# Re-ordered attention and maxout kernel: part of W loaded ahead of batch 1's x, single PSUM banks, padded x for every state read

## The chip, the cores and the metric

One core of one Trainium2 chip runs the program. The metric is device microseconds of one execution, as the median of several runs; less is better.

## The reference

Eight batches (B = 8) of attention between x and 32 state vectors per head, in both directions, and then a feed-forward layer whose hidden value is the largest of three products. H = 8 heads, S = 512 tokens, Ns = 32 states, D = 64.

```python
x:     (8, 8, 512, 64)      state: (8, 8, 32, 64)
a  = softmax(x @ state^T / 8, over the states);  xread = a  @ state     # 512 rows a batch
a2 = softmax(state @ x^T / 8, over the tokens);  sread = a2 @ x         # 32 rows a batch
y = concat([xread, sread], rows), heads side by side                    # (8*544, 512)
h = max(y @ w1, y @ w2, y @ w3)                                         # (8*544, 768)
out = h @ w_out                                                         # (8*544, 512), float32
```

## The kernel before

**What is computed where.** xread is never built. For a batch b the kernel multiplies each head's 32 states by the matching 64 rows of w1, w2, w3 ahead of time: G[b] holds state @ W for all heads, 128 rows (4 heads of 32 states) by 2 parities of heads by 3 matrices by 768 columns. Layer 1 is then aT @ G: for each of the six slices m of 128 hidden columns, `maxout` (L473) runs three PSUM banks (one for each matrix) of two 128x512 matmuls each. `max_first` (L489) copies the first bank to SBUF on ACT, `max_second` (L494) and `max_third` (L499) take the maximum with the second and the third bank on DVE, and the last writes ht. Layer 2 (L511) multiplies 128 tokens of ht by w_out in six 128x512 matmuls, `layer2_out` copies the bank to osb, and `store` sends osb to DRAM.

**The steps of a batch**, by the names that the plan uses: x is loaded with a cast to bf16 by POOL's DMA queue (`lx`; `lxg` loads the four even or odd heads only; `lxu` and `cxu` load uncast and cast on DVE, for batch 0's first half). x is turned to xT on TensorE (`xt`, with the copy `xtc`) for batches 0 and 1, and by a transposing DMA on SP's queue (`xtd`) for the rest. `sc` makes the scores (16 matmuls, or 8 for one parity), `ex` takes exp on ACT, `sum` adds over the states and inverts on DVE, `wt` multiplies (on POOL, 128x1024, or on DVE), giving a. a is turned by TensorE and a copy (`at`, `atc`) in batches 0 and 1, by DMA on SP's queue (`atd`) in the others. `sr` reads x by e for the 32 state rows (32 matmuls that use 32 columns of the array each), `srs` divides, `srt` turns the result by DMA on SP's queue, `ap` copies it to its place in atp, from which `l1s` makes the states' rows of layer 1 at the end. The states themselves are loaded in pairs of batches (`lst`), cast twice over (`stc`), turned (`stt` on TensorE) and copied into a block-diagonal tile bd (`stp`).

**G** is made by small matmuls on a quarter of the array, 64x32 (`g_mm`, L424): `g b m` makes slice m of all three matrices for batches 0 and 1, since W comes in slice by slice; `gr b c0 c1` makes 512 columns of the 2304 for the later batches, and `gq` 256. They are emptied by `gc`, `grc` and `gqc`.

**PSUM.** Four banks (tags b0 to b3) go to everything that takes one bank, in the order of the digits of BANKS. The other four are two pairs (w0, w1): `two_banks` gives a pair to `g`, to `gr` and to the scores of batches 2 to 7, and one instruction of 128x768 or 128x1024 empties the pair.

**sread's right side.** In batches 2 to 7 `pad` (L370) copies x on POOL into a tile xp with 65 columns a head, the 65th a one, so that one matmul of 65 columns gives the sum of e as well. In batches 0 and 1 the matmul takes 128 columns: 64 of x, and 64 ones that lie behind x in x_sb, by a hand-made address pattern (L389).

**What sets the order.** PLAN (L18) is a list of steps that one table of functions carries out; every engine does its own instructions in the order of that list, and waits only for its operands and for its buffer. BANKS, PAIRS and PLACES say which buffer each step takes. Each DMA stands in the queue of the engine that issues it (S is SP, P is POOL, A is ACT). `busy` is one matmul of zeros; these stand on TensorE ahead of the first use of W. At the end `look`, `flag` and `vl` test whether any sum left its range, in which case a second, safe program runs; `hold` is a matmul and a copy behind the last layer-2 copy.

In the plan the batches overlap: batch b's layer 1 stands with batch b-1's layer 2 and with batch b+1's G. The beginning is different: batches 0 and 1 are done together, slice by slice, as W lands.

Of the kernel before, what the change touches and what calls it, by code (L numbers as in the profile page):

```python
# [9 lines left out]
F32 = mybir.dt.float32  # L10
# [8 lines left out]
    lst 0 A; lxu 0 0 S; zero; clr 0; clr 1; clr 2; clr 3; warm; lxg 0 1; busy 1; xones 1; ident; busy 1;  # L19
    lxg 1 0; busy 1; busy 1; stc 0 D; busy 1; busy 1; busy 1; busy 1; busy 1; lxg 1 1; stt 0; busy 1; busy 1;  # L20
    cxu 0 0 D; xt 0 0; stp 0 A; busy 1; xt 0 1; lw 0 2 1; lw 0 1 0; xtc 0 0 D; sc 0 0; xones 0; lw 0 2 2;
    xtc 0 1 D; busy 1; busy 1; sc 0 1; xt 1 0; ex 0 0; ex 0 1; lw 1 3 0; sum 0 0; sum 0 1; xtc 1 0 A; busy 1;
    busy 1; xt 1 1; sc 1 0; xtc 1 1 D; ex 1 0; busy 1; busy 1; sc 1 1; lw 2 3 2; wt 0 1 D; lw 2 3 1; lw 3 4 0;
    wt 0 0 P; lw 3 6 2; at 0 0; sr 0; ex 1 1; sr 1; g 0 0; sum 1 0; wt 1 0 P; g 1 0; atc 0 0 A; at 0 1; at 1 0;
    gc 0 0 A; atc 0 1 A; g 1 1; sum 1 1; gc 1 0 D; atc 1 0 A; srs 0; srs 1; g 0 1; wt 1 1 P; at 1 1; gc 0 1 A;
    l1 0 0; atc 1 1 D; lst 1 A; m0 0 0; lst 3 A; gc 1 1 A; ma 0 0; lw 3 6 1; lw 4 6 0; lxg 2 1; lxg 2 0; l1 0 1;
    m0 0 1; lwo; mb 0 0; g 0 2; g 1 2; ma 0 1; l1 1 0; lst 2 A; gc 0 2 A; mb 0 1; m0 1 0; ma 1 0; l1 0 2;
    mb 1 0; gc 1 2 A; m0 0 2; ma 0 2; l1 1 1; m0 1 1; g 1 3; stc 1 P; mb 0 2; ma 1 1; g 0 3; mb 1 1; stt 1;
    gc 1 3 A; l1 1 2; gc 0 3 A; m0 1 2; stp 1 DA; ma 1 2; g 0 4; g 0 5; l1 0 3; gc 0 5 D; g 1 4; mb 1 2;
    gc 0 4 A; m0 0 3; gc 1 4 A; ma 0 3; gr 2 1792 2304; mb 0 3; l1 1 3; m0 1 3; grc 2 1792 2304 A; xtd 2;  # L30
    ma 1 3; l1 0 5; stc 2 P; g 1 5; gr 2 0 512; mb 1 3; m0 0 5; ma 0 5; l1 1 4; gc 1 5 A; gr 2 1280 1792;
    m0 1 4; grc 2 0 512 D; mb 0 5; gr 2 512 1024; ma 1 4; grc 2 1280 1792 AD; l1 0 4; m0 0 4; ma 0 4; stt 2;
    mb 0 4; sc 2 -; ex 2 -; grc 2 512 1024 D; stp 2 AD; stc 3 D; mb 1 4; l2 0 3; l2 0 0; l2c 0 3 A; l2c 0 0 A;
    sum 2 -; l2 0 1; ones; pad 2; lxg 3 0; lxg 3 1; wt 2 - P; stt 3; xtd 3; l2c 0 1 A; l1 1 5; pad 3;
    so 0 0 2 P; lx 4; m0 1 5; l2 0 2; ma 1 5; mb 1 5; stp 3 A; l2c 0 2 A; l2 1 0; gq 2 1024 1280; gr 3 0 512;
    gr 3 1792 2304; l2c 1 0 D; grc 3 1792 2304 D; gqc 2 1024 1280 A; grc 3 0 512 A; atd 2; sr 2; l2 1 1; srs 2;
    sc 3 -; l1 2 0; m0 2 0; ex 3 -; l2c 1 1 D; l2 1 3; ma 2 0; gq 3 1024 1280; so 0 2 4 P; gqc 3 1024 1280 A;
    l2c 1 3 A; gr 3 512 1024; gr 3 1280 1792; mb 2 0; sum 3 -; wt 3 - P; atd 3; xtd 4; srt 0; sr 3; srs 3;
    l1 2 1; m0 2 1; ma 2 1; l1 2 2; m0 2 2; mb 2 1; ma 2 2; l1 2 3; m0 2 3; mb 2 2; ma 2 3; l1 2 5; m0 2 5;
    mb 2 3; l2 1 2; grc 3 1280 1792 A; grc 3 512 1024 A; ma 2 5; mb 2 5; l2c 1 2 D; l1 2 4; so 1 2 4 P; m0 2 4;  # L40
    ma 2 4; lx 5; mb 2 4; so 1 0 2 P; pad 4; gr 4 1792 2304; gr 4 0 512; grc 4 1792 2304 AD; l2 2 0; l2 2 1;
    grc 4 0 512 D; l2c 2 0 A; l1 3 0; m0 3 0; sc 4 -; ex 4 -; xtd 5; l2c 2 1 D; l2 2 3; ma 3 0; gq 4 1024 1280;
    gr 4 1280 1792; gr 4 512 1024; mb 3 0; sr 4; gqc 4 1024 1280 A; sum 4 -; srs 4; l2c 2 3 A; l1 3 1; m0 3 1;
    ma 3 1; l1 3 2; m0 3 2; mb 3 1; ma 3 2; l1 3 3; m0 3 3; mb 3 2; ma 3 3; l1 3 5; wt 4 - P; m0 3 5; mb 3 3;
    l2 2 2; grc 4 1280 1792 A; grc 4 512 1024 A; ma 3 5; mb 3 5; l2c 2 2 D; l1 3 4; so 2 2 4 P; m0 3 4; ma 3 4;
    lx 6; mb 3 4; atd 4; srt 1; ap 0 A; so 2 0 2 P; pad 5; gr 5 1792 2304; gr 5 0 512; grc 5 1792 2304 AD;
    l2 3 0; l2 3 1; grc 5 0 512 D; l2c 3 0 A; l1 4 0; m0 4 0; sc 5 -; ex 5 -; xtd 6; l2c 3 1 D; l2 3 3; ma 4 0;
    gq 5 1024 1280; gr 5 1280 1792; gr 5 512 1024; mb 4 0; sr 5; gqc 5 1024 1280 A; sum 5 -; srs 5; l2c 3 3 A;
    l1 4 1; m0 4 1; ma 4 1; l1 4 2; m0 4 2; mb 4 1; ma 4 2; l1 4 3; m0 4 3; mb 4 2; ma 4 3; l1 4 5; wt 5 - P;
    m0 4 5; mb 4 3; l2 3 2; grc 5 1280 1792 A; grc 5 512 1024 A; ma 4 5; mb 4 5; l2c 3 2 D; l1 4 4; so 3 2 4 P;  # L50
    m0 4 4; ma 4 4; lx 7; mb 4 4; atd 5; srt 2; ap 1 A; so 3 0 2 P; pad 6; gr 6 1792 2304; gr 6 0 512;
# [20 lines left out]
    l2p 7 1 128 384; sop 7 2 0 128 A; l2p 7 0 256 384; l2pc s 0 0 256 A; l2pc 7 1 128 384 A; l2c s 1 D;  # L72
    l2p 7 1 384 512; l2p 7 0 128 256; sop 7 3 0 256 S; sop 7 2 128 384 P; l2pc 7 0 256 384 D; sop 7 1 128 384 A;
    l2pc 7 1 384 512 D; sop 7 1 384 512 A; l2pc 7 0 128 256 D; sop 7 0 128 256 A; sos 1 S; sop s 0 0 256 S;
    sop 7 0 256 384 S; hold; vl;
"""

BANKS = """
# [665 lines left out]
```

## Time and profile before

| | us |
|---|---|
| runs of the kernel (3): lowest, median, highest | 152.44, 152.61, 152.64 |
| span of the profiled execution | 150.5 |
| what lies around that span (median less span) | 2.1 |
| TensorE busy | 145.1 (96%) |
| VectorE (DVE) busy | 118.0 (78%) |
| ScalarE (ACT) busy | 83.2 (55%) |
| GpSimd (POOL) busy | 56.1 (37%) |

Times in the trace count from the start of the span. PE is TensorE's matmuls, PEld its weight loads. The granted TensorE clock was 1.000 over the span. A row of the chain of waits has a start, a length and what the time went to; a row of a timeline has a start, a length, the engine and the line, and in brackets how long that engine had been idle and what ended it. The length of a group of matmuls runs to the end of the last one, which overlaps with the next group; differences of starts don't have that overlap.

### The profile page before, as it was taken

The page shows a single profiled execution, that of the slowest core. Times are in us where ns is not written, and L with a number is a line of the kernel's source. Part 1 is how long each engine was busy: PE and PEld are TensorE (multiplying, and loading weights), DVE is VectorE, ACT ScalarE, POOL GpSimd, SP SyncE. Part 2 cuts the span into 40 slices and gives each one's busy share as a digit, 9 for nine tenths or more (in the row PEclk, how much of TensorE's full clock was granted, in tenths as well). Part 3 has the DMA queues.
Part 4 walks back from the last instruction along what each step waited for, and adds up shares of the span by engine and source line. Part 5 has one row for each costly group of instructions (what it writes and reads, how often), then busy time and mean ns, then how long its engine had stood idle before and what let it go on. Part 6 is the DMA issues. An engine that isn't in the chain of part 4 may idle for free.

```text
span 150.5 us, 3618 instructions
## 1 busy us (share of the span) xinstructions
PE 145.1 (96%) x1422; PEld 72.8 (48%) x1422; DVE 118.0 (78%) x202; ACT 83.2 (55%) x144; POOL 56.1 (37%) x78
## 2 busy tenths in 40 slices
PE   6998999999999999999999999999999999999991
PEld 2556443335444443444344434443444446689770
DVE  6488788999967899789978997899789888674443
ACT  3366888965654574457546764676466653332220
POOL 6996911090392507350735064506250200001500
PEclk9999999999999999999999999999999999999999
DMA  4999999949647996998399839983303340300555
GB/s 121 195 188 189 206 230 198 196 97 139 124 97 171 235 182 189 108 209 178 145 102 216 183 139 90 231 183 131 157 4 78 121 175 7 139 0 17 190 199 167
DMA packets 39108, 22.29 MB, mean 148 GB/s; under 512 B 23072, under 2 KB 36896, under 8 KB 39088
## 3 DMA queue, kind: packets, MB, share of 16 engines
q0 software_dynamic: 15872, 13.96, 49.3%
q1 hardware_dynamic: 21632, 6.69, 22.8%
q10 hardware_dynamic: 1584, 1.38, 3.2%
q8 instruction: 12, 0.20, 0.6%
q14 instruction: 8, 0.07, 0.2%
HBM read 15.20 MB, written 8.91 MB: 160 GB/s over the span
## 4 chain that ended last, share of the span: by engine, by line
PE 88%; DMA 5%; POOL 3%; issue 1%; DVE 1%; ACT 1%; POOLq 0%
PE pw L477 47%; PE po L514 25%; PE pg L427 6%; DMA w<-in_moe_w_dram 5%; PE po L532 4%; PE ps L305 2%; PE psr L391 2%; POOL w L217 1%; POOL x L206 1%; PE pgh L427 1%; ACT G L444 1%; PE pt L261 1%; DVE held L593 0%; PE idle L591 0%; PE pat L358 0%
## 5 line engine op out<-in xcount | busy, mean ns | idle before, releaser
L477 PE MATMUL pw<-aT,G 128*128 128x512 bf16 x288 | 66.7, 379 | 0.0
L492 ACT CAST t<-pw 128x512 bf16<-128x512 f32 (+1 forms) x54 | 30.5, 564 | 27.3 <-PE pw L477 26.4
L497 DVE TENSOR_TENSOR t<-t,pw 128x512 bf16<-128x512 bf16 (+1 forms) x54 | 35.3, 654 | 11.1 <-ACT t L492 8.9
L477 PEld LDWEIGHTS <-G 128*128 128x128 bf16 x288 | 27.1, 98 | 32.8 <-issue 2.1
L514 PE MATMUL po<-wout,ht 128*128 128x512 bf16 x168 | 39.7, 379 | 0.0
L505 DVE TENSOR_TENSOR ht<-t,pw 128x512 bf16<-128x512 bf16 x48 | 32.9, 686 | 4.5
L349 POOL TENSOR_TENSOR a<-e,rden 128x1024 bf16<-128x1024 bf16 (+1 forms) x9 | 14.6, 1622 | 27.2 <-ACT osb L526 11.1
L514 PEld LDWEIGHTS <-ht 128*128 128x128 bf16 x168 | 15.4, 98 | 19.0 <-issue 1.7
L548 POOL DMA_DIRECT2D out_dram<-osb x13 | 7.4, 571 | 27.5 <-ACT t L492 27.5
L466 ACT CAST G<-pg 128x1024 bf16<-128x1024 f32 (+1 forms) x17 | 14.7, 895 | 2.1 <-PE pg L427 2.1
L526 ACT COPY osb<-po 128x512 f32<-128x512 f32 x15 | 8.9, 592 | 9.1 <-PE po L514 9.1
L526 DVE COPY osb<-po 128x512 f32<-128x512 f32 x14 | 9.6, 688 | 3.9 <-PE po L514 3.8
L375 POOL COPY xp<-x 128x1024 bf16<-128x1024 bf16 x12 | 12.3, 1059 | 0.0
L313 ACT ACTIVATE e<-ps 128x1024 bf16<-128x1024 f32 (+1 forms) x10 | 8.5, 854 | 6.7 <-PE ps L305 6.7
L466 DVE CAST G<-pg 128x1024 bf16<-128x1024 f32 (+1 forms) x12 | 11.6, 995 | 0.0
L342 DVE TENSOR_REDUCE seen<-e 128x32 f32<-128x1024 bf16 (+1 forms) x10 | 10.0, 997 | 1.7 <-ACT e L313 1.7
L427 PE MATMUL pg<-w,bd 64*32 64x512 bf16 (+1 forms) x288 | 10.7, 362 | 0.4 <-DMA w<-in_moe_w_dram 0.2
L444 ACT CAST G<-pg 128x768 bf16<-128x768 f32 x10 | 8.0, 810 | 2.7 <-PE pg L427 2.5
L543 POOL DMA_DIRECT2D out_dram<-osb x4 | 2.2, 544 | 19.4 <-ACT osb L537 19.4
L249 PE MATMUL idle<-zero 128*128 128x512 bf16 x18 | 7.4, 506 | 1.8 <-DVE zero L225 1.3
L477 PE MATMUL pw<-atp,w 128*128 128x256 bf16 x72 | 8.7, 272 | 0.0
L217 POOL DMA_DIRECT2D w<-in_moe_w_dram x10 | 7.7, 782 | 0.0
(70 smaller groups left out, 112.1 us busy)
## 6 DMA issues: line engine op xcount, KB each, us to landing
out_dram<-osb POOLq DMA_DIRECT2D x12, 512.0 KB, 3.7
x<-in_x_dram POOLq DMA_DIRECT2D x4, 512.0 KB, 7.2
x<-in_x_dram POOLq DMA_DIRECT2D x7, 256.0 KB, 5.8
w<-in_moe_w_dram POOLq DMA_DIRECT2D x4, 256.0 KB, 7.5
w<-in_moe_w_dram POOLq DMA_DIRECT2D x2, 384.0 KB, 7.5
wout<-in_moe_w_out_dram POOLq DMA_DIRECT2D x1, 768.0 KB, 12.0
out_dram<-osb SPq DMA_DIRECT2D x3, 256.0 KB, 2.4
stf<-in_state_dram ACTq DMA_DIRECT2D x4, 128.0 KB, 5.3
```

The lines of the kernel that those rows point to most:

```text
L342: nc.vector.reduce_sum(out=den, in_=parity(e[b], g), axis=AX.X)
L349: times[c](out=parity(a[b], g).rearrange("p j g s n -> p j (g s) n"), in0=parity(e[b], g).rearrange("p j g s n -> p j (g s) n"), in1=rdens ...
L375: nc.gpsimd.tensor_copy(out=xp[b][:, :, :, g * (D + 1):g * (D + 1) + D], in_=v[:, g])
L427: nc.tensor.matmul(p(s, g), bd(b, 2 * s + g)[64 * g:64 * g + 64, g, :], f(w_sb[64 * g:64 * g + 64, s]), start=True, stop=True, tile_positi ...
L444: copier[c[g]](out=G[b][:, g:h, :, m * 128:m * 128 + 128], in_=p[:, g:h, 0:384].rearrange("p g (i f) -> p g i f", i=3))
L466: copier[c[g]](out=v[:, g:h], in_=p[:, g:h, 0:c1 - c0])
L477: nc.tensor.matmul(pw[i][:, 0:n], lhs(i, k), rhs(k), start=(k == 0), stop=(k == nk - 1))
L492: nc.scalar.copy(out=t0s[b, m][:, 0:n], in_=open_ps["l", b, m][0][:, 0:n])
L497: nc.vector.tensor_max(t1s[b, m][:, 0:n], t0s.pop((b, m))[:, 0:n], open_ps["l", b, m][1][:, 0:n])
L505: nc.vector.tensor_max(ht[b][:, m, :], t1s.pop((b, m))[:, 0:n], open_ps.pop(("l", b, m))[2][:, 0:n])
L514: nc.tensor.matmul(p, ht[b][:, m, tokens(b, j)], wout_sb[:, m, :], start=(m == 0), stop=(m == NM - 1))
L526: copier[c[i]](out=o[:, j, i * w:i * w + w], in_=p[:, i * w:i * w + w])
```

## The change

- **The order.** PLAN is replaced as a whole, and with it BANKS and PLACES. PLAN has 30 `busy` in place of 18.
- **W in smaller pieces, earlier.** 14 loads in place of 10. The first, slice 1 of w1, is issued ahead of both halves of batch 1's x; the next two bring slices 0 and 1 of w2 and w3, then slice 0 of w1. The first G is that of slice 1, and layer 1 begins with slice 1 of batch 0.
- **Single banks.** `two_banks` and PAIRS are gone. All eight banks are in one row of digits; what took a pair takes two banks, and two instructions (128x512, or 128x384 in `gc`) empty them: on ACT and DVE half and half where the plan has AD or DA.
- **Padded x for all batches.** `pad` gets an engine (batch 0 on ACT, the rest on POOL), writes two ones in one memset, and is done for batches 0 and 1 too; `sread` loses its 128-column form, and `xones` is gone.
- **States 2 to 5** (pairs 1 and 2) are turned by a DMA on SP (`std`) in place of `stt`. Their cast, on POOL before, is on ACT.
- **Batch 4's e** is made turned (`sq`: 16 matmuls of a 64x32 quarter with 256 columns; `eq`: two exps) and turned back by DMA (`etd`), in place of `sc` and `ex`.
- **Stores** are 21 `so` in place of 16, on ACT, SP and POOL where they were nearly all POOL's; batch 0's come late in the program.
- The exp that warmed ACT up at the beginning (`warm`) stands in the middle now.

```diff
-    lst 0 A; lxu 0 0 S; zero; clr 0; clr 1; clr 2; clr 3; warm; lxg 0 1; busy 1; xones 1; ident; busy 1;
-    lxg 1 0; busy 1; busy 1; stc 0 D; busy 1; busy 1; busy 1; busy 1; busy 1; lxg 1 1; stt 0; busy 1; busy 1;
...
+    zero; lst 0 A; lxg 0 1; ident; lxu 0 0 S; busy 1; lw 1 2 0; busy 1; busy 1; lxg 1 1; stc 0 D; clr 0; lxg 1
+    0; busy 1; busy 1; busy 1; busy 1; busy 1; stt 0; cxu 0 0 D; busy 1; busy 1; busy 1; busy 1; stp 0 A; lw 0 2
...
     def bank(shape, dtype, name):
-        return pp.tile(shape, dtype, tag="b" + next(homes["b"]), bufs=1, name=name)
-
-    def two_banks(shape, dtype, name):
-        return pp.tile(shape, dtype, tag="w" + next(homes["w"]), bufs=1, name=name)
+        return pp.tile(shape, dtype, tag="b" + next(homes[0]), bufs=1, name=name)
...
     def exps(b, g=None):
         new(e, b, [128, J, 2, HS, Ns], "e")
-        nc.scalar.activation(
-            out=parity(e[b], g).rearrange("p (c i) g s n -> p i c (g s n)", i=2),
-            in_=open_ps.pop(("s", b, g)).rearrange("p (i c) g s n -> p i c (g s n)", i=2),
-            func=AF.Exp, scale=scale)
+        out = parity(e[b], g).rearrange("p (c i) g s n -> p i c (g s n)", i=2)
+        ps = open_ps.pop(("s", b, g))
+        if g is None:
+            for i in range(2):
+                nc.scalar.activation(
+                    out=out[:, i], in_=ps[i].rearrange("p c g s n -> p c (g s n)"), func=AF.Exp, scale=scale)
...
-    def pad(b):
+    def pad(b, c="P"):
         new(xp, b, [128, HS, J, 2 * D + 2], "xp")
-        nc.gpsimd.memset(xp[b][:, :, :, D:D + 1], 1.0)
+        {"D": nc.vector, "P": nc.gpsimd, "A": nc.gpsimd}[c].memset(xp[b][:, :, :, D:D + 2], 1.0)
         v = xv[b].rearrange("p (s g) j d -> p g s j d", g=2)
         for g in range(2):
-            nc.gpsimd.tensor_copy(out=xp[b][:, :, :, g * (D + 1):g * (D + 1) + D], in_=v[:, g])
+            copier[c](out=xp[b][:, :, :, g * (D + 2):g * (D + 2) + D], in_=v[:, g])
...
-                    if b in xp:
-                        both = xp[b][:, s, j, g * D:g * D + D + 1]
-                    else:
-                        xj = xv[b][:, 2 * s + g, j, :]
-                        both = bass.AP(xj.tensor, xj.offset,
-                                       (xj.ap[0], (XW - ((2 * s + g) * J + j) * D, 2), (1, D)))
                     nc.tensor.matmul(
-                        p[32 * s:32 * s + 32, g], e[b][:, turned(j), g, s, :], both,
+                        p[32 * s:32 * s + 32, g], e[b][:, turned(j), g, s, :],
+                        xp[b][:, s, j, g * (D + 1):g * (D + 1) + D + 1],
...
     def g_sliced(b, m, c):
         new_g(b)
-        p = open_ps.pop(("g", b, m))
-        for g, h in ((0, 2),) if len(c) == 1 else ((0, 1), (1, 2)):
-            copier[c[g]](out=G[b][:, g:h, :, m * 128:m * 128 + 128],
-                         in_=p[:, g:h, 0:384].rearrange("p g (i f) -> p g i f", i=3))
+        for g, p in enumerate(open_ps.pop(("g", b, m))):
+            copier[c[g % len(c)]](out=G[b][:, g, :, m * 128:m * 128 + 128],
+                                  in_=p[:, 0:384].rearrange("p (i f) -> p i f", i=3))
```

POOL's queue at the beginning, before (x_82 is batch 0's x, x_83 batch 1's; the first load of w is slices 0 and 1 of w2, the second slice 0 of w1, the third slices 0 and 1 of w3):

```order
L206 DMA x_82<-in_x_dram 128x4x256
L236 MEMSET x_83 128x64
masks.py:197 MEMSET ident 128x128
masks.py:199 ISA
masks.py:199 AFFINE_SELECT ident<-ident 128x128
L206 DMA x_83<-in_x_dram 128x4x256 x2
L217 DMA w<-in_moe_w_dram 128x4x256
L217 DMA w<-in_moe_w_dram 128x4x128
L236 MEMSET x_82 128x64
L217 DMA w<-in_moe_w_dram 128x4x256 x2
L217 DMA w<-in_moe_w_dram 128x4x128 x3
L349 TENSOR_TENSOR a<-e,rden 128x4x128
```

One load of 128 columns of W has moved ahead of batch 1's x. Behind it the same queue now, the first load of w being slice 1 of w1:

```order
L203 DMA x_82<-in_x_dram 128x4x256
masks.py:197 MEMSET ident 128x128
masks.py:199 ISA
masks.py:199 AFFINE_SELECT ident<-ident 128x128
L214 DMA w<-in_moe_w_dram 128x4x128
L203 DMA x_83<-in_x_dram 128x4x256 x2
L214 DMA w<-in_moe_w_dram 128x4x256 x2
L214 DMA w<-in_moe_w_dram 128x4x128
L377 MEMSET xp 128x16x2
L214 DMA w<-in_moe_w_dram 128x4x128 x4
L214 DMA w<-in_moe_w_dram 128x4x256
L354 TENSOR_TENSOR a<-e,rden 128x4x128
```

Up to and with the last load that the first G needs (that of w3), both queues hold three halves of x, 256 columns of w2, 128 of w1 and 256 of w3.

SP's queue in the middle of the program, before (stores by POOL's queue are not in it; from batch 2's a on):

```order
L366 DMA_TRANSPOSE aT<-a 128x8x128 x2
L291 DMA_TRANSPOSE xT<-x_86 128x16x128
L410 DMA_TRANSPOSE ats<-sr 128x128
L291 DMA_TRANSPOSE xT<-x_87 128x16x128
L366 DMA_TRANSPOSE aT<-a 128x8x128
L410 DMA_TRANSPOSE ats<-sr 128x128
```

The same stretch now: a store, the second pair of states and batch 4's e are in it, and four turns of sread stand in a row ahead of batch 5's a.

```order
L371 DMA_TRANSPOSE aT<-a 128x8x128
L259 DMA_TRANSPOSE stT<-st 128x4x128
L528 DMA out_dram<-osb 128x512
L285 DMA_TRANSPOSE xT<-x_86 128x16x128
L371 DMA_TRANSPOSE aT<-a 128x8x128
L404 DMA_TRANSPOSE ats<-sr 128x128
L340 DMA_TRANSPOSE e<-eT 128x8x128
L285 DMA_TRANSPOSE xT<-x_87 128x16x128
L371 DMA_TRANSPOSE aT<-a 128x8x128
L285 DMA_TRANSPOSE xT<-x_88 128x16x128
L404 DMA_TRANSPOSE ats<-sr 128x128 x4
L528 DMA out_dram<-osb 128x512 x2
```

The store waits for a copy of layer 2's result, and everything behind it in the queue waits with it.

ACT's instructions behind the load of the second pair of states, before (t is `max_first`'s result, stf the loaded states):

```order
L190 DMA stf_75<-in_state_dram 128x256
L492 CAST t_423<-pw_412 128x512
L190 DMA stf_77<-in_state_dram 128x256
L444 CAST G<-pg 128x6x128
L492 CAST t_442<-pw_433 128x512
L190 DMA stf_76<-in_state_dram 128x256
L444 CAST G<-pg 128x6x128
L492 CAST t_479<-pw_467 128x512
```

No cast of the states is among them. The same place now:

```order
L187 DMA stf_75<-in_state_dram 128x256
L472 CAST t_451<-pw_441 128x512
L437 CAST G<-pg 128x3x128
L367 COPY aT<-pat 128x4x128
L472 CAST t_476<-pw_465 128x512
L472 CAST t_510<-pw_501 128x512
L437 CAST G<-pg 128x3x128 x2
L472 CAST t_523<-pw_514 128x512
L250 CAST st<-stf_75 128x512
```

The cast of st stands between two of ACT's layer-1 copies and waits for the load at the head of these rows.

More of the change, by code (lines that the diff above doesn't have):

```diff
@@ L34 @@
[L34 to L48, printed above, removed]
@@ L165 @@
     open_ps = {}
-    homes = {n: iter("".join(t.split())) for n, t in (("b", BANKS), ("w", PAIRS))}
+    homes = [iter("".join(BANKS.split()))]
     places = {}
@@ L299, in scores @@
     def scores(b, g=None):
+        if g is None:
+            ps = [bank([128, 2, 2, HS, Ns], F32, "ps") for _ in range(2)]
+        else:
+            p = bank([128, J, 1, HS, Ns], F32, "ps")
+            ps = [p[:, 2 * i:2 * i + 2] for i in range(2)]
+        open_ps["s", b, g] = ps if g is None else [p]
         gs = (0, 1) if g is None else (g,)
-        p = open_ps["s", b, g] = (two_banks if g is None else bank)([128, J, len(gs), HS, Ns], F32, "ps")
         for jj in range(2):
@@ L686 @@
                 a_turned(b, g, c)
-            if b >= 2:
-                pad(b)
+            pad(b)
             sread_below_max(b)
```

230 lines of the change are left out of this document (114 added, 116 removed), and 4 rows, old and new, of the table BANKS.

## The prediction, as it was put on record

> **What bounds the kernel now.** I read the page first (busy shares, slices), then the chain of waits in order of time, then TensorE's timeline, then the groups of instructions by shape, and last the transfers.
>
> ```profile
> PE 145.1 (96%) x1422; PEld 72.8 (48%) x1422; DVE 118.0 (78%) x202; ACT 83.2 (55%) x144; POOL 56.1 (37%) x78
> PE   6998999999999999999999999999999999999991
> DVE  6488788999967899789978997899789888674443
> DMA  4999999949647996998399839983303340300555
> ```
>
> TensorE has work in every slice but the first and the last ones. The chain shows how much of that is the path.
>
> ```profile
> 6.06 7.41 DMA w<-in_moe_w_dram
> ...
> 13.60 0.40 PE pg L427 x8
> ...
> 14.02 0.81 ACT G L444
> ...
> 14.88 0.68 PE pg L427 x16
> 15.55 0.33 PE pat L358 x4
> 15.88 2.59 PE pw L477 x12
> ...
> 34.06 0.22 PE pt L261 x4
> 34.29 0.47 PE ps L305 x16
> ...
> 38.64 0.22 PE pt L261 x4
> ...
> 48.48 0.43 PE pg L427 x16
> 48.92 0.38 PE psr L391 x32
> ...
> 144.29 2.67 PE po L532 x36
> ...
> 146.98 0.30 DVE osb L537
> ```
>
> Until 13.47 (6.06 + 7.41) the chain is the arrival of W. From 13.60 to 146.96 (144.29 + 2.67), so for 133.4 us, it is TensorE with one exception of 0.81 us, an eviction on ACT. Behind 146.96 stand the last copy, the last store and the end of the program: 150.5 - 146.96 = 3.5 us. So the time is the arrival of W, plus the matmuls owed from there on, plus TensorE's stalls, plus 3.5. The page's span is 150.5; the median of the runs is 152.61, and I carry the 2.1 between them over unchanged. About 0.2% (0.3 us) is what a measurement of this kernel can tell from no change.
>
> **The change, part by part.**
>
> *Start (a): estimate -0.3, from -0.6 to +0.5.* The bytes ahead of the first usable slice are as they were (three halves of x, 640 columns of W), so W lands at 13.5 again; the piece that moved ahead of batch 1's x trades places with it. From 13.60 to the first layer 1 at 15.88 stand 2.28 us, of which TensorE worked 0.40 + 0.68 + 0.33 = 1.41. At most the other 0.87 can be won. G's slice is now emptied by DVE and ACT at once, 384 columns each:
>
> ```profile
> L444 ACT CAST G<-pg 128x768 bf16<-128x768 f32 x10 | 8.0, 810 | 2.7 <-PE pg L427 2.5
> L466 ACT CAST G<-pg 128x1024 bf16<-128x1024 f32 x12 | 11.7, 1024 | 0.0
> L466 ACT CAST G<-pg 128x512 bf16<-128x512 f32 x5 | 2.9, 586 | 2.1 <-PE pg L427 2.1
> L469 ACT CAST G<-pgh 128x256 bf16<-128x256 f32 x12 | 3.9, 375 | 3.8 <-PE pgh L427 3.8
> L313 ACT ACTIVATE e<-ps 128x1024 bf16<-128x1024 f32 x6 | 6.1, 1025 | 4.2 <-PE ps L305 4.2
> L286 ACT COPY xT<-pxt 128x1024 bf16<-128x1024 bf16 x1 | 1.0, 1012 | 0.0
> ```
>
> Midway between 375 and 586 is 0.48 in place of 0.81: 0.33 sooner. Against it, batch 0's softmax starts later: `pad 0 A` puts two copies of 1.01 on ACT ahead of the first exp. Hence the upper end; the lower one is two thirds of 0.87, since the last `at` still waits for POOL's multiplication.
>
> *Work that slips behind the start (b): +0.39.* sread of batch 1 (0.38 by the row of 32 psr), half of batch 1's scores (half of 0.47) used to run while W was awaited, and now run after; one group of pat (0.22, the price of the equal four transposes of pt) goes the other way. 0.38 + 0.23 - 0.22.
>
> *States turned by DMA (c): -0.44.* Two groups of pt at 0.22 leave TensorE. What hides the DMA: between pair 1's cast and the first `gr 2` stand five steps of layer 1 on TensorE, 6.5 us at 1.29 each. In that time the turn must land, and POOL must copy it to bd, behind two pads and w_out's load in its queue. If the cover goes, what the pair is late is lost at `gr 2`.
>
> *Batch 4's turned scores (d): -0.1, from -0.24 to 0.* 16 matmuls of a 64x32 quarter with 256 columns replace 16 of 64 columns (0.47). No such matmul exists before; the nearest are pg's, 16 with 512 columns in 0.43. Half of that gives 0.22; counting each 256 at 0.23, as the chain gives eight pgh, no gain.
>
> *Changes between the whole array and its quarters (e): +0.23, from 0 to +0.3.*
>
> ```profile
> 54.44 1.46 PE L514 MATMUL po<-wout,ht 128*128 128x512 bf16 x6
> 55.73 1.46 PE L477 MATMUL pw<-aT,G 128*128 128x512 bf16 x6
> 57.12 0.63 PE L427 MATMUL pg<-w,bd 64*32 64x512 bf16 x16
> 57.68 2.76 PE L514 MATMUL po<-wout,ht 128*128 128x512 bf16 x12
> 42.75 0.23 PE pgh L427 x8
> ```
>
> By differences of starts, six wide matmuls cost 1.29 (54.44 to 55.73), but 1.39 when a quarter group follows (55.73 to 57.12), and the group 0.56 (57.12 to 57.68) where the same 16 inside a group cost 0.43. So each group costs 0.10 + 0.13 = 0.23 beyond its work. Behind the first G the plan had 18 such groups and has 19: batch 0's and 4's pieces stand more singly, and other groups merge. The Trainium skill, TensorEngine Tiling (Array Packing), section Key Properties, says that a change of tiling mode drains TensorE. It speaks against every G step put alone, and the 0.23 here agrees with it; the sum would have 0 without it.
>
> *Stalls while batches 0 and 1 run (f): -0.15, from -0.45 to +0.3.*
>
> ```profile
> 23.70 1.36 PE pw L477 x6
> 25.50 1.45 PE pw L477 x6
> 30.71 1.40 PE pw L477 x6
> 32.66 1.40 PE pw L477 x6
> ```
>
> Against 1.29 these four hold 0.07 + 0.16 + 0.11 + 0.11 = 0.45 too much, of which up to 0.10 each is the price of a group that follows. With eight banks for all, TensorE can run two steps of layer 1 ahead of DVE; before, three of four banks were one step. I take a third.
>
> *Evictions in two (g): 0.* Two of 586 for one of 1024 on ACT are 0.15 more. Some 28 such on ACT make 4.2 us, on an engine that is busy for 83 of 150: hidden, unless a copy of layer 1 queues behind them. The Trainium skill, ScalarE: Activation LUTs, section What ACT_TABLE_LOAD costs, gives about 93 ns as the overlap of activations that follow each other, so 0.055 net for each split and 1.5 us in all by its figure; the sum holds 0 by either.
>
> *Narrower sread (h): 0.* Batch 0's stands ahead of W's arrival. Batch 1's is the 0.38 in (b).
>
> *The rest: 0, from -0.2 to +0.4.* Behind batch 1's layer 2 the same matmuls stand in another order, and before, they ran there without a gap in the chain: nothing to win, only to lose. The end is alike: one copy behind the last matmul, then a store; `flag` now stands behind all copies.
>
> Sum: -0.3 + 0.39 - 0.44 - 0.1 + 0.23 - 0.15 = -0.37. Span 150.1, time 152.2.
>
> **The rivals.**
>
> *R1, banks set TensorE free (faster).* All of the 0.45 in (f) and 0.6 of (a) go: -0.3 - 0.3 beyond the sum, 151.6. For it: DVE shows 9 in slices 8 to 11. Against: 6, 7 and 8 follow.
>
> *R2, the start gives nothing.* The exps behind `pad 0 A` hold batch 0's a back, (a) is 0: 152.5. For it: by the order, ACT had nothing between the states' copies and the first exp before.
>
> *R3, slower: a state's cast holds ACT up.* ACT's cast of pair 1 waits in line for a load that ACT issued eight instructions before, and the layer-1 copies of batches 0 and 1 queue behind it, then DVE's maxima, then TensorE for a bank.
>
> ```profile
> POOL st L256 <- DMA stf<-in_state_dram: 4.8, 2, 2.9
> stf<-in_state_dram ACTq DMA_DIRECT2D x4, 128.0 KB, 5.3
> L492 ACT CAST t<-pw 128x512 bf16<-128x512 f32 x48 | 28.2, 588 | 23.1 <-PE pw L477 22.9
> DMA to landing us min/median/max: 2.8/5.3/6.5
> xT<-x SPq DMA_TRANSPOSE x6, 5.3
> aT<-a SPq DMA_TRANSPOSE x6, 2.9
> ```
>
> (The row of min, median and max is that of the states' loads; the last two are turns by DMA, for R4.) POOL, which did these casts before, waited 4.8 us in two. On ACT there stand four copies at 588, three halves of G at 0.48 and one aT (0.59) between load and cast: 4.4 us, against 5.3 to landing. ACT would wait 0.9; with the second such cast, whose load has four such instructions and so 2.4 us of work behind it, up to 2.9 more if it too takes 5.3. Whatever TensorE cannot bridge from its banks is lost. It decides against the forecast when TensorE loses over 0.7; at 1.2 the time is 153.4. Against it: the second load falls near 37 us, by slices 11 and 12, where DMA was 6 and 4 tenths busy, and the quickest state load took 2.8.
>
> *R4, slower: batch 4's e comes late.* Between `sq` and `sr 4` TensorE has one run of G (0.22), three groups of 1.29 and three runs (0.75 with the change of mode): 4.8 us. The detour takes two exps at 0.6 and one turn of a's shape, 2.9: 4.1. Margin 0.7. With xT's 5.3 the wait would be 1.7, and the time 153.9; it is slower than before from a turn of 4.3 us on.
>
> **How the numbers follow.** Forecast 0.44 (of it 0.29 faster by over 0.3 us, 0.14 within, 0.01 slower: its own range is 151.9 to 152.6, and 152.2 is just past the bound of 152.3), R1 0.17 (faster), R2 0.14 (0.01 faster, 0.11 within, 0.02 slower), R3 0.15 and R4 0.10 (slower). Faster 0.47, same 0.25, slower 0.28. The lower end is R1 with a little of (e)'s lower bound, 151.3; the upper is R3's 153.4, which leaves out R4 and the tails.
>
> **What would show it.** Right: the first layer-1 matmuls start near 15.6; two groups of pt are left on TensorE; groups of pg carry the same 0.23; layer 2 of batch 1 starts some 0.3 us earlier than before, and from there to the last matmul the distance is as it was. R1: the four rows of 1.36 to 1.45 are at 1.29 everywhere. R2: the first layer 1 at 15.9. R3: ACT's cast of st is idle before it for over 0.5 us by a state's DMA, and a gap on TensorE's row follows. R4: psr of batch 4 waits for e's DMA. I would be wrong if TensorE shows idle time behind 45 us, or if W's first slice lands later than 13.5.

## The result and the profile after

The changed kernel takes 164.44 us (median of 6 runs, from 162.32 to 173.16), the kernel before 152.31 beside it (6 runs, 151.96 to 152.64). The ratio is 1.069, with a 95% interval from 1.064 to 1.074: 7% slower, where 152.2 was forecast. The profiled execution has a span of 163.6 us at a granted clock of 0.979; three of the six have 160.5 to 161.9 us at 0.989, and the ratio and its interval go by these three alone.

The page of the changed kernel: busy shares, and the slices that answer to those shown of before.

```profile
PE 149.1 (91%) x1409; PEld 74.6 (46%) x1426; DVE 112.7 (69%) x208; ACT 88.6 (54%) x174; POOL 57.8 (35%) x77
...
PE   6998999819997799999998999999999999999990
...
PEclk9999999995999699999999999999999999999999
DMA  4999999998559719949299739209301469005453
```

TensorE's row now has a 1 and two 7s, and the clock's row a 5 and a 6 just where the work comes back: 1.000 before, 0.979 now. The chain of waits says what TensorE waited for (start, length, what):

```profile
16.50 1.29 PE pw L457 x6
...
24.66 9.60 DMA stT<-st
34.31 1.05 POOL bd L265
35.41 1.05 POOL bd L265
36.51 0.62 PE pg L421 x15
...
38.28 1.91 PE po L494 x4
...
45.65 1.91 POOL a L354
47.58 6.74 DMA aT<-a
54.36 2.72 PE pw L457 x6
...
78.04 1.91 POOL a L354
79.97 6.37 DMA aT<-a
86.38 1.46 PE pw L457 x6
...
156.03 2.97 PE po L512 x36
```

Before, no DMA stood in the chain behind the arrival of W. Now three do, all of them turns by DMA on SP's queue, and each takes two to over three times the 2.9 us that the prediction quoted for aT. The waits of TensorE, in all, times, longest:

```profile
PE pg L421 <- POOL bd L265: 4.0, 2, 3.3
PE pw L457 <- DMA aT<-a: 3.2, 2, 2.3
```

What was in flight with the first of them, by the transfers issued from 24 to 36 us (KB, us to landing):

```profile
wout<-in_moe_w_out_dram POOLq DMA_DIRECT2D x1, 768.0 KB, 10.2
stT<-st SPq DMA_TRANSPOSE x1, 9.6
xT<-x SPq DMA_TRANSPOSE x1, 9.9
...
```

w_out's load was issued at 24.38, 0.28 us ahead of the states' turn, and the two landed within 0.3 us of each other. The second turn (aT at 47.58) went out 0.07 us behind a 512 KB load of batch 4's x, the third within 1 us of two such loads.

The difference of the two spans is 163.6 - 150.5 = 13.1 us. Of it the rows hold: first layer 1 at 16.50 and not 15.88, 0.6; idle time in front of batch 2's first run of G, 4.0; four matmuls behind it in 1.91 where four take 0.86, 1.05; idle time in front of batch 2's first layer 1, 2.3; that layer 1 in 2.72 instead of 1.29, 1.4, and the scores behind it 0.85 instead of 0.47, 0.4; idle time at batch 4's, 0.9; from the last layer-2 matmul to the end 163.6 - 159.0 = 4.6 instead of 3.5, 1.1. Together 11.8; the other 1.3 are in none of these rows. A second execution of the changed kernel (`after_again` below: span 161.9, clock 0.989) has the same two waits, so they don't belong to this one alone.

### The profile page after: what moved, and what is told of

Read it like the earlier page. It is cut to its first block, busy times and chain, and to the rows that moved or that the text cites. A ratio compares the mean times of both kernels' runs of the same rounds, so it can differ in the third digit from the quotient of the medians.

```text
span 163.6 us, 3639 instructions
## 1 busy us (share of the span) xinstructions
PE 149.1 (91%) x1409; PEld 74.6 (46%) x1426; DVE 112.7 (69%) x208; ACT 88.6 (54%) x174; POOL 57.8 (35%) x77
## 4 chain that ended last, share of the span: by engine, by line
PE 72%; DMA 14%; POOL 4%; DVE 3%; ACT 2%; issue 1%; DVEq 0%; POOLq 0%; ACTq 0%
PE pw L457 36%; PE po L494 17%; DMA aT<-a 8%; DMA stT<-st 6%; PE idle L243 5%; PE pg L421 5%; PE po L512 4%; POOL a L354 3%; PE ps L304 2%; DVE seen L347 1%; POOL bd L265 1%; PE psr L389 1%; PE pxt L272 1%; PE pat L363 1%; ACT e L316 1%
## 5 line engine op out<-in xcount | busy, mean ns | idle before, releaser
L477 DVE TENSOR_TENSOR t<-t,pw 128x512 bf16<-128x512 bf16 (+1 forms) x54 | 34.8, 654 | 21.3 <-ACT t L472 13.1
L449 ACT CAST G<-pg 128x512 bf16<-128x512 f32 (+1 forms) x42 | 20.5, 555 | 9.9 <-PE pg L421 9.7
L421 PE MATMUL pg<-w,bd 64*32 64x512 bf16 (+2 forms) x336 | 12.4, 359 | 4.0 <-POOL bd L265 4.0
L449 DVE CAST G<-pg 128x512 bf16<-128x512 f32 (+1 forms) x18 | 10.8, 630 | 5.0 <-PE pg L421 5.0
L243 PE MATMUL idle<-zero 128*128 128x512 bf16 x28 | 10.0, 483 | 1.3 <-DVE zero L222 1.3
L214 POOL DMA_DIRECT2D w<-in_moe_w_dram x14 | 10.8, 785 | 0.7 <-DMA x<-in_x_dram 0.7
L421 PEld LDWEIGHTS <-bd 64*32 64x32 bf16 x336 | 3.8, 90 | 12.4 <-issue 7.2
L437 ACT CAST G<-pg 128x384 bf16<-128x384 f32 x19 | 8.4, 504 | 1.7 <-PE pg L421 1.7
L528 POOL DMA_DIRECT2D out_dram<-osb x3 | 1.8, 589 | 20.1 <-DVE hts L485 20.1
L506 DVE COPY osb<-po 128x512 f32<-128x512 f32 x10 | 6.9, 686 | 1.1 <-PE po L494 1.0
L457 PEld LDWEIGHTS <-w 128*128 128x128 bf16 x72 | 7.0, 98 | 1.2
```

The costliest lines, as they stand in the source:

```text
L243: nc.tensor.matmul(p, zero[:, 0:128], zero, start=True, stop=True)
L421: nc.tensor.matmul(p(s, g), bd(b, 2 * s + g)[64 * g:64 * g + 64, g, :], f(w_sb[64 * g:64 * g + 64, s]), start=True, stop=True, tile_positi ...
L449: copier[c[g % len(c)]](out=v[:, g, c0:c1], in_=p[:, 0:c1 - c0])
L457: nc.tensor.matmul(pw[i][:, 0:n], lhs(i, k), rhs(k), start=(k == 0), stop=(k == nk - 1))
L477: nc.vector.tensor_max(t1s[b, m][:, 0:n], t0s.pop((b, m))[:, 0:n], open_ps["l", b, m][1][:, 0:n])
L506: copier[c[i]](out=o[:, j, i * w:i * w + w], in_=p[:, i * w:i * w + w])
```

## The experiments

Theory A: a turn by DMA that has a load beside it lands late, and the plan now puts three turns on the path beside loads. Rival B: TensorE is held by its banks and by DVE, which empties them, and the turns only cover that. Rival C: the turns are slow in this program by themselves (their place on SP's queue, their shape). Runs of one set share a chip and the runs of before; sets stand on different chips, so across sets I compare ratios. Where an edit adds or drops a step that takes a bank, BANKS is adjusted with it; that isn't printed.

### One edit at a time

**The states of pair 1 on TensorE** (`pair1_tensor`).

```diff
-    ... ma 0 5; std 1; mb 1 1; gc 0 4 A; g 1 4; mb 0 5; ... pad 2 P; stp 1 P; gr 2 1280 1792;
+    ... ma 0 5; mb 1 1; gc 0 4 A; g 1 4; stt 1; mb 0 5; stp 1 DA; ... pad 2 P; gr 2 1280 1792;
```

> The changed kernel with one edit: the states of pair 1 are turned on TensorE again and placed by DVE and ACT; pair 2 stays on the DMA. In the changed kernel that DMA took 9.60 us beside the loads of x and w_out (24.66 to 34.26), TensorE then sat idle for 3.3 and 0.7 us at the first run of G for batch 2, and POOL, which waited with the copy to bd, issued batch 3's x only at 36.40. Theory A (a turn by DMA that shares its time with loads is late, and its wait is passed on along POOL's and SP's queues): both idle stretches go, and with them the stretch at a lower granted clock behind them, 5 us in all, less 0.2 for the four transposes: about 157.5, from 156.5 to 159. Batch 3's x is issued near 31. Rival B (TensorE is held by its banks and by POOL's pads, and the DMA wait only covers that): under 1 us, 161.5 to 162.5, with an idle stretch left before 37 us.

Measured: 162.41 us, ratio 1.067 (1.059 to 1.075). Nothing like 157.5: theory A missed by 4 to 5 us. Its waits of TensorE:

```profile
PE pw L457 <- DMA aT<-a: 4.4, 2, 2.6
PE pg L421 <- DVE ht L485: 1.7, 1, 1.7
...
PE pt L255 <- DVE ht L485: 0.7, 1, 0.7
```

The waits for DVE are what B spoke of, but they could be my edit's: the transposes took a bank that DVE had yet to empty, and the copies to bd stood ahead of its maxima. I tried a better place below. And the turn of batch 2's a took 6.82 us again, beside the load.

**Batch 4's x behind the pads** (`x4_later`).

```diff
-    srs 2; lx 4; pad 3 P; l2 1 1;
+    srs 2; pad 3 P; lx 4; l2 1 1;
```

> The changed kernel with one edit: on POOL, the load of batch 4's x stands behind batch 3's two pad copies, not ahead of them, so it is issued some 2.2 us after the turn of batch 2's a (47.58) and not beside it. Theory A (sharing with a load makes the turn slow): batch 2's aT takes about 3 us instead of 6.74, as in the kernel before where nothing was loaded at that time; the 2.3 us of idle TensorE at 52 and the half-speed layer 1 behind it (2.72 us where six matmuls take 1.29) go: 158.5, from 158 to 160.5. Rival C (a turn takes 6 to 10 us in this program whatever stands beside it, for its place in SP's queue): aT stays at 6 to 7 us and the time at 162.4.

Measured: 161.35 us, ratio 1.058 (1.050 to 1.065), so less was won than the expectation had, which already left pair 1's wait in (3.6 us here). The changed kernel wasn't run on this chip, and its ratio was 1.069 on one chip and 1.081 on another (`after_again`), so how much this edit is worth in time isn't settled; the row of the turn is the result. The transfers issued from 48 to 51 us:

```profile
x<-in_x_dram POOLq DMA_DIRECT2D x1, 512.0 KB, 6.7
aT<-a SPq DMA_TRANSPOSE x1, 3.0
...
```

The load now goes out 1.9 us behind the turn, and the turn takes 3.03 us instead of 6.74. TensorE's layer 1 follows without a gap at full rate:

```profile
51.28 1.47 PE L494 MATMUL po<-wout,ht 128*128 128x512 bf16 x6
52.58 1.46 PE L457 MATMUL pw<-aT,G 128*128 128x512 bf16 x6
```

Rival C falls at this place: one swap on POOL's queue, with nothing changed on SP's, more than halves the turn.

**x of batches 6 and 7 behind the pads** (`x67_later`).

```diff
-    wt 4 - P; lx 6; xtd 5; ma 3 2; lx 7; pad 5 P; atd 4;
+    wt 4 - P; xtd 5; ma 3 2; pad 5 P; lx 6; lx 7; atd 4;
```

> The changed kernel with one edit: the loads of batches 6 and 7 of x stand behind batch 5's two pad copies on POOL, not around them, so they are issued some 2 us after the turn of batch 4's a and not with it. Theory A: that aT takes about 3 us instead of 6.37 and the 0.88 us of idle TensorE at 85.5 goes: 161.5, from 161 to 162. Rival C (the turn is slow by itself): aT stays over 6 us and the time at 162.4. Whether the idle 0.88 had a share in the clock is not expected: no slice there shows less than full.

Measured: 160.62 us, ratio 1.058 (1.051 to 1.066). The turn of batch 4's a takes 3.08 us instead of 6.37, and its wait is gone. More is gained than the 0.9 expected, but this run's profile also has pair 1's turn at 8.21 and its wait at 2.7 where the changed kernel had 9.60 and 4.0. What is not the edit's in the time I can't say; the row of the turn is the result.

**w_out's load later** (`wout_later`).

```diff
-    m0 0 5; lwo; g 0 4; ... pad 2 P; stp 1 P;
+    m0 0 5; g 0 4; ... pad 2 P; lwo; stp 1 P;
```

> The changed kernel with one edit: the load of w_out, 768 KB, is issued behind batch 2's pad copies, near 29 us, not at 24.4. It is meant for one row alone: the turn of pair 1's states, issued at 24.66, now stands beside the end of two loads of batch 2's x (to 27.1) and no other. Theory A: it lands near 28.5 to 30 (4 to 5 us) instead of 34.26. Rival C (9 us belong to this turn by itself, whatever runs beside it): it lands at 33 or later. The time is not the question: w_out arrives some 5 us later, and batch 0's layer 2 waits for it, so that what is won at the states is lost there.

Measured: 168.84 us, one run. The transfers issued from 24 to 29.5 us, and TensorE's first wait:

```profile
stT<-st SPq DMA_TRANSPOSE x1, 3.7
xT<-x SPq DMA_TRANSPOSE x1, 4.3
```

```profile
PE po L494 <- DMA wout<-in_moe_w_out_dram: 5.8, 1, 5.8
```

The states' turn lands at 28.43, 3.66 us after its issue, and the wait for bd shrinks from 4.0 to 0.5. So 9.6 us is not the length of this turn. The price is the one that was announced: batch 0's layer 2 waits 5.8 us for w_out. The order of the loads can't simply be turned about.

### Pair 1 again, and all three edits

**The changed kernel on this chip** (`after_again`, no edit).

> The changed kernel as it is, on the chip that the other three of this set run on, as the mark for them: in the first set one of three single edits that should have given 0.9 us gave 160.6, so the kernel itself may stand lower than 162.4 on another chip. All theories: 160.5 to 163, with idle stretches of TensorE near 33, 52 and 85 us.

Measured: 163.88 us, ratio 1.081 (1.073 to 1.088), 0.9 above what was expected. Its waits of TensorE:

```profile
PE pg L421 <- POOL bd L265: 4.5, 2, 3.8
PE pw L457 <- DMA aT<-a: 3.6, 2, 2.5
```

The turns behind them took 10.08 us (states) and 6.92 (batch 2's a).

**Pair 1 on TensorE, earlier** (`pair1_early`).

```diff
-    gc 1 3 DA; g 0 5; gc 0 5 A; l1 1 1; ... ma 0 5; std 1; mb 1 1; ... pad 2 P; stp 1 P;
+    gc 1 3 DA; g 0 5; stt 1; gc 0 5 A; stp 1 DA; l1 1 1; ... ma 0 5; mb 1 1; ... pad 2 P;
```

> The changed kernel with the states of pair 1 turned on TensorE, placed better than in the first try: right behind slice 5 of batch 0's G, in a bank that is empty by then, with the copies to bd on DVE and ACT behind that slice's. In the first try the four transposes waited 0.7 us for a bank, and the first run of G for batch 2 then 1.7 us for DVE's maximum. Theory A (the late turn was the loss, and the rest was the bank that I took): the idle 4 us near 33 go and nothing takes their place over 0.5 us: 3.5 to 5 us below the changed kernel on this chip. Rival B (behind the wait for the states stood a wait of nearly that length for DVE, which empties the banks of batches 0 and 1): TensorE still waits 1 to 2 us for DVE between 28 and 36 us, and 1.5 to 2.5 us are won. By both, the turn of batch 2's a still shares its time with a load, and TensorE still waits there.

Measured: 161.74 us, ratio 1.064 (1.057 to 1.070): 2 us won, not 3.5 to 5. By the time alone that would be rival B. TensorE's timeline says otherwise (in brackets its idle time):

```profile
31.52 0.79 PE L421 MATMUL pg<-w,bd 64*32 64x384 bf16 x24
32.32 0.45 PE L389 MATMUL psr<-xp,e 128*32 128x65 bf16 x32
...
34.66 1.47 PE L457 MATMUL pw<-aT,G 128*128 128x512 bf16 x6
38.55 0.64 PE L304 MATMUL ps<-bd,xT 128*128 128x64 bf16 x16 [2.42 <-DMA xT<-x]
```

No wait for DVE is left: the last of batches 0 and 1 and the first run of G for batch 2 are one group of 24. B falls; the waits of the first try were its own. A new wait has come 4 us later, for the turn of batch 2's x, which took 12.2 us: with bd ready early, POOL issued batch 3's x at 28.2 and not at 36.2 as in `after_again`, and so beside that turn.

**All three** (`all_apart`): pair 1 as in the last run, and both loads of x behind the pads.

> The changed kernel with all three edits: pair 1's states on TensorE as in the run before, batch 4's x loaded behind batch 3's pad copies, x of batches 6 and 7 behind batch 5's. Theory A: the turns of the a of batches 2 and 4 take about 3 us, TensorE has no idle stretch over 0.5 us behind 36 us, the granted clock is full: 153 to 154.5, so within 1 to 2 us of the kernel before (what is left: the first layer 1 some 0.3 to 0.6 later and 1.0 more behind the last matmul). If over 156, there is a loss that these three places do not hold.

Measured: 154.71 us in one run and 158.68 to 161.82 in the other three (median 158.76). By the median, "over 156, there is a loss that these three places do not hold" is the branch it took; one run of four is 0.2 us above the range expected. The profile is of a run of 158.84. In it the aT's of batches 2 and 4 take 3.07 and 3.03, and the one wait left behind 20 us is this:

```profile
PE ps L304 <- DMA xT<-x: 2.7, 1, 2.7
```

### The other direction, in the kernel before

**Batch 4's x earlier in the kernel before** (`before_x4_early`).

```diff
-    wt 2 - P; stt 3; xtd 3; l2c 0 1 A; l1 1 5; pad 3; so 0 0 2 P; lx 4;
+    wt 2 - P; lx 4; stt 3; xtd 3; l2c 0 1 A; l1 1 5; pad 3; so 0 0 2 P;
```

> The kernel before with one edit, the counterpart of the one that helped the changed kernel: the load of batch 4's x is issued right behind POOL's multiplication for batch 2 (near 41.9) and so beside the turn of batch 2's a, not 2.6 us after it. Theory A: that turn takes 6 to 7 us instead of 2.71, the first layer 1 of batch 2, which starts at 45.50, waits some 3 us for it, and part of what follows runs at half the granted clock: 155 to 156.5. Rival C (loads beside a turn do not matter, the changed kernel's queue on SP does): the turn stays near 2.7 and the time at 152.0.

Measured: 159.43 us, ratio 1.046 (1.040 to 1.053): 7.3 us slower by one moved load, more than the 3 to 4.5 expected. The transfers issued from 41.9 to 44 us, and TensorE's timeline:

```profile
x<-in_x_dram POOLq DMA_DIRECT2D x1, 512.0 KB, 8.2
aT<-a SPq DMA_TRANSPOSE x1, 8.3
```

```profile
45.20 0.63 PE L305 MATMUL ps<-bd,xT 128*128 128x64 bf16 x16
50.53 2.72 PE L477 MATMUL pw<-aT,G 128*128 128x512 bf16 x6 [4.69 <-DMA aT<-a]
53.04 2.45 PE L514 MATMUL po<-wout,ht 128*128 128x512 bf16 x6
```

The turn takes 8.34 us instead of 2.71 and TensorE waits 4.69; then six matmuls take 2.72 instead of 1.29, and the next six end 2.24 later instead of 1.29. That is 4.69 + 1.43 + 0.95 = 7.1, all of the difference of the spans (157.6 - 150.5); the expectation had the waiting about 1.7 too short and the stretch at half rate too cheap. Theory A makes a fast kernel slow with it, without any other part of the change.

### The fourth place, the clock and the end

**Batch 3's x behind w_out's arrival** (`xT2_clear`): `all_apart` with one edit more.

```diff
-    sc 2 -; lxg 3 1; lxg 3 0; ex 2 -; l2c 0 0 A; l2 0 3; ones; warm;
+    sc 2 -; ones; lxg 3 1; lxg 3 0; ex 2 -; l2c 0 0 A; l2 0 3; warm;
```

> The run with all three edits and one more: on POOL, the copy that waits for w_out stands ahead of the two loads of batch 3's x, not behind them (as in the kernel before), so these loads are issued near 32 and not at 28.7. In the run with three edits their early start had put them beside the turn of batch 2's x, which took 12.38 us (26.78 to 39.17; 5.70 in the kernel before), and TensorE waited 2.7 us for it at batch 2's scores. Theory A: that turn now lands at 32 to 35, no idle stretch of TensorE over 0.5 us is left behind 16 us, the granted clock is full, and the time is 153 to 154: about 1.0 above the kernel before for the end and up to 0.6 for the start. If a further turn comes late, or the time stays over 155, the three or four places were not all.

Measured: 155.01 us (154.19 to 156.18), ratio 1.019 (1.015 to 1.023). That is just past the 155 named in the expectation, and 1 us above the range of theory A. The turn of batch 2's x lands at 34.74 and its wait is gone; all of TensorE's waits now:

```profile
PE idle L243 <- DVE zero L222: 1.3, 1, 1.3
PE pt L255 <- DVE st L250: 1.2, 1, 1.2
PE pat L363 <- POOL a L354: 0.3, 1, 0.3
```

Four moved steps take the ratio from 1.069 (1.081 on another chip) to 1.019. No run is quicker than the one of 154.71 with three edits; what the fourth place changes is that all six runs now lie between 154.19 and 156.18. The first row belongs to the beginning; the 1.2 is a load of states that came late.

**Zeros in the gaps** (`busy_in_gaps`): the changed kernel with matmuls of zeros where TensorE waited.

```diff
-    stp 1 P; gr 2 1280 1792; ... l2 1 1; l1 2 0;
+    stp 1 P; busy 13; gr 2 1280 1792; ... l2 1 1; busy 8; l1 2 0;
```

> The changed kernel with 13 matmuls of zeros on TensorE ahead of the first run of G for batch 2 (where it sat idle for 3.3 to 3.8 us) and 8 ahead of batch 2's first layer 1 (2.3 to 2.5 us), shorter than the waits. They compute nothing. Theory (the granted clock falls because TensorE is idle, and the half-speed stretch behind is a second price of the same wait): the clock stays at 1.00, the waits stay as long as before, and the time falls by the 1.8 to 3.4 us that the clock of 0.989 to 0.979 stands for: 160.5 to 162 where the changed kernel has 163.9 on such a chip and 162.4 on another. Rival (the clock falls for another reason, the load of the whole chip say): clock and time as in the changed kernel.

Measured: 161.61 us, ratio 1.066 (1.062 to 1.069), clock 0.995 to 1.000. Its clock by slices, and what follows the filled gap (by the chain, six matmuls in 1.40 and not four in 1.91):

```profile
PEclk9999999999999999999999999999999999999997
```

```profile
31.66 2.98 PE L243 MATMUL idle<-zero 128*128 128x512 bf16 x13
34.69 0.63 PE L421 MATMUL pg<-w,bd 64*32 64x512 bf16 x16
35.25 0.45 PE L389 MATMUL psr<-xp,e 128*32 128x65 bf16 x32
35.63 1.47 PE L494 MATMUL po<-wout,ht 128*128 128x512 bf16 x6
```

The turns are as slow as ever (stT 8.0, aT 7.0), but the clock no longer falls: the half rate was a second price of the same waits. In time this shows only against the 1.081 of the other chip; against 1.069 the intervals overlap. The Trainium skill, TensorE: Matmul & The Clock Gate, Part 1, lets the clock halve after at least one idle window of about 3.4 us. The traces agree as to the cause; but here 2.31 us of idle time halved it in one execution, while 2.37 us in `x67_later` and 2.49 in `after_again` did not.

**The flag** was tried three times: `flag_early` and `mended` move it ahead in the repaired kernel, `before_flag_late` back in the kernel before.

```diff
 flag_early (on xT2_clear)
-    l2p s 0 256 512; l2p 7 1 128 384; ... sop 7 0 384 512 P; flag;
+    l2p s 0 256 512; flag; l2p 7 1 128 384; ... sop 7 0 384 512 P;
 mended (on xT2_clear; also lst 3 A, from behind grc 2 512 1024 AD to behind stc 1 A)
-    mb s 3; l1s 5; ... sop 7 0 384 512 P; flag;
+    mb s 3; flag; l1s 5; ... sop 7 0 384 512 P;
 before_flag_late (on the kernel before)
-    l2p 7 3 0 256; flag; ... l2pc 7 0 128 256 D; sop 7 0 128 256 A;
+    l2p 7 3 0 256; ... l2pc 7 0 128 256 D; flag; sop 7 0 128 256 A;
```

> The run before this one and one more edit: the test of the sums (a matmul and two small DVE instructions that write the flag) stands three groups of layer 2 earlier, not behind the last copy but one. In the changed kernel the engines read the flag at 159.5 to 159.8, after the last copies, and the span ends 4.5 us behind the last matmul of layer 2; in the kernel before, with the flag written 7 us ahead of the end, 3.5. Theory (the flag is on the path at the end): 0.5 to 1.1 us below the run before this one. Rival (the end is set by the last stores alone): no change beyond 0.2.

Measured: 156.85 us, ratio 1.032 (1.029 to 1.035), 1.8 slower than its neighbour. DVE stood idle 2.07 us at the flag with the last copies behind it, so this says nothing of the flag.

> The kernel with the four edits that keep turns and loads apart (155.0 us, from 154.2 to 156.2) with two more: the flag is computed ahead of the last states' slice of layer 1, in a bank that is empty there, so that no copy queues behind it (in the try before this one, DVE waited 2.07 us for it with the copies of the last layer 2 behind it, and these stores landed late); and the load of the last pair of states is issued by ACT some 10 us earlier, since in the profile of the 155.0 kernel TensorE waited 1.2 us for its cast. Theory (the reading of the flag stands on the path at the end of the changed kernel): the distance from the last matmul to the end of the span goes from 4.6 to 3.5 to 4.0, and the time is 153.3 to 154.3. Rival (stores alone set the end): distance 4.6, time 154.2 to 155.

Measured: 155.20 us, ratio 1.021 (1.018 to 1.025): no gain on 155.01. Its last layer-2 matmul ends at 147.69 and the span at 152.9, so the end has grown to 5.2, against both theories: the last two stores now take 3.9 and 3.8 us where they took 2.1 and 2.0.

> The kernel before with one edit: the computing of the flag moves from 7 us ahead of the last matmul to behind the last copy, where the changed kernel has it. Theory (reading the flag is on the path when it stands that late): 0.5 to 1.1 us slower than before, 152.7 to 153.3, and the distance from the last matmul to the end goes from 3.5 to 4.0 to 4.6. Rival (stores alone set the end): no change beyond 0.2.

Measured: 156.05 us, ratio 1.025 (1.023 to 1.028): 3.9 us slower, four times what was expected. The last layer-2 matmul ends at 146.37, so the distance to the end is 7.4 and not 4.0 to 4.6: the loss lies behind it. Who reads the flag and when, in this run (span 153.8; the row of min, median and max in ns, then first and last start) and in the kernel before (span 150.5):

```profile
L583 SPq TENSOR_LOAD <-flag x1: 660/660/660, 147.0 to 147.0; - x1
L583 POOLq TENSOR_LOAD <-flag x1: 672/672/672, 147.0 to 147.0; - x1
```

```profile
L583 POOLq TENSOR_LOAD <-flag x1: 795/795/795, 140.7 to 140.7; - x1
L583 SPq TENSOR_LOAD <-flag x1: 700/700/700, 147.1 to 147.1; - x1
```

SP's read stands where it stood; POOL's comes 6.3 us later, and the span ends 6.8 us behind it. Behind its read POOL goes through closing steps that the views leave out, since they are not counted as work; in the trace's instruction records the longest is a DRAIN of 3.25 us. It starts at 149.66 here and at 146.36 in the kernel before, and the span ends 0.85 behind its end in both. So with the flag early these steps are for the most part hidden behind the last matmuls and stores. In the changed kernel all engines read the flag at 159.5 to 159.8, the last stores land at 161.4, and the end is 4.1 behind POOL's read. There the DRAIN is 1.04 long, and the span again ends 0.84 behind its end. Why it is shorter there isn't shown; it means that the 3.9 can't be carried over to the changed kernel.

**Batch 4's scores as in the others** (`mended_sc4`).

```diff
-    sq 4; ... eq 4; ... etd 4;
+    sc 4 -; ... ex 4 -; ...
```

> The run before this one, with batch 4's e made as in the other batches (scores of 128 rows and two exps) and not turned twice over, so one DMA fewer on SP's queue. By the step of the prediction that gave the turned scores 0.1 us of gain, from nothing to 0.24: 0 to 0.24 slower than the run before this. Rival (the detour costs: its run of quarter-size matmuls stands alone and pays the change of tiling, and e comes back 3.2 us late): 0.2 to 0.6 faster.

Measured: 155.67 us, ratio 1.024 (1.020 to 1.027), beside 1.021 (1.018 to 1.025) without it. Not faster, so the rival falls; 0.5 us slower in the medians, with intervals that overlap.

## Why the prediction was wrong, point by point

**(a) Start, -0.3: nothing was won.** W's first slice landed at 13.50 as said; by the chain the first layer 1 started at 16.50, where 15.6 was forecast and 15.88 was before. By the timeline, which has these starts 0.16 earlier, it was 15.49 to 16.66 in all executions with this beginning, and 15.14 to 15.90 in three with the old one. The first G started at 14.82 and not 13.60, behind eight transposes that waited 0.6 us for POOL's multiplication. That is R2's time, 0 or worse. Its cause isn't shown, and this profile speaks against it: behind the pads ACT stood idle for 0.55 us until the scores were there, so the pads didn't hold the first exp.

**(c) States by DMA, -0.44: the step that failed.** The cover was worked out right in kind ("If the cover goes, what the pair is late is lost at `gr 2`"), but a late pair had no term in the sum and no chance among the rivals. I set 6.5 us against a turn, gave the turn no length, and named w_out's load only as something ahead of POOL in its queue, not as traffic that the turn would share. The turn took 9.60 and POOL's two copies 2.14: 4.0 us were lost at `gr 2`, and 1.0 to the clock behind it. With w_out's load out of the way it was 3.66, and the cover would nearly have held (0.5 left).

**"The rest: 0": the second step that failed.** I looked at the same matmuls in another order and found nothing to win. What the order had moved was loads: that of batch 4's x from behind the turn of batch 2's a to 0.07 us ahead of it, and those of batches 6 and 7 beside batch 4's turn. I had checked each queue's own order, and not which transfers of different queues would now be in flight together. The kernel before had a hint of it: its turns of sread's rows, issued at 55.40 and 70.11, took 4.1 and 2.3 us, the first beside a load of x and stores, the second with no load beside it.

```profile
ats<-sr SPq DMA_TRANSPOSE x1, 4.1
```

```profile
ats<-sr SPq DMA_TRANSPOSE x1, 2.3
```

**"The end is alike": wrong by 1.1.** I saw that `flag` stood behind all copies and gave it no price. `before_flag_late` shows that its place alone can cost 3.9 in the kernel before. In the changed kernel POOL's steps behind its late read set the end; but with the flag early nothing was won, since the last stores then took longer (`mended`).

**(d) Turned scores, -0.1:** in line with what was measured (about -0.5, with intervals that overlap). **(b), (e), (f), (g):** not to be told apart. By the chain, TensorE takes 147.69 - 15.76 = 131.93 us from the first layer 1 to the last matmul in `mended`, against 146.94 - 15.88 = 131.06 before, at a clock of 1.00 in both (the 0.995 of that run's span is lost behind the last matmul). That is 0.9 more, where these four terms, (d), and the half of (c) that `mended` still has add up to +0.15. Which of them was too low isn't shown.

**The rivals.** R1 could not show beside losses of this size. R3 had the right pair of states and the wrong transfer: the casts were on time, the turn behind them was not. R4 looked for the loss at batch 4's e, whose turn took 3.2 us against a limit of 4.3; the loss at batch 4 was its a. Both rivals priced turns at what they take alone or beside little. "I would be wrong if TensorE shows idle time behind 45 us" was the test that decided.

**What stays open.** Why the last stores take 3.8 us once the flag is early, and so whether the end of the changed kernel can be had back; 1.3 us of the profiled difference and some 0.7 of `mended`'s; and why one run of `all_apart` took 154.71, since its profile wasn't kept. No version here beats the kernel before.

## What to carry to other kernels

When a plan is re-ordered, list for each DMA on the path which transfers of all queues will be in flight with it, not only what stands ahead of it in its own: a load that moves by 2 us on POOL's queue can double or triple a turn on SP's. A turn with a consumer on the path goes out ahead of bulk loads, by placing the load behind work of its queue; here 1.9 us of such work was enough for a turn of 3.0. A mended wait lets the next load start sooner, so the list is made anew after each edit.

## What the runs showed of the hardware

- A turn of a, 3.0 to 3.4 us with the load issued about 2 us behind it, took 6.4 to 8.3 with a 512 KB load issued with it; one of x, 4.3 with only a load of states beside it, took 12.4 beside loads of w_out, x and states. The Trainium skill, DMA: Bandwidth & Descriptors, Queues, rings and completion order, says that each DMA engine takes turns between queues by packets; that fits a turn that slows down beside a load, and the size of it is only in these rows. All of these loads go by POOL's queue with a cast, but for the states'; whether other transfers slow a turn as much was not tried.
- Idle time of TensorE was paid twice: after 4.69 us, six matmuls took 2.72 us where six at full rate behind a wait took 1.47; behind idle stretches of 2.3 to 2.7 us it came out either way.
- From POOL's read of the flag to the end there were 6.8 us in the kernel before with a late flag, and 4.1 in the changed one, with a DRAIN of 3.25 and of 1.04 us between; with the flag read early, these steps were done before the last stores had landed in `mended`, and ended 0.5 us behind the last store in the kernel before.
